# Output products of a recurrent attention kernel: accumulating by 128-column groups over all heads, without a sum over head groups

## The chip, the cores and the metric

The kernel runs on one core of a Trainium2 chip. The metric is the device time of one execution in microseconds (us); lower is better. Executions of one kernel differ by up to about 1% here. Ratios are the mean time of one kernel's runs over the mean of the other's of the same rounds, so they are not quite the ratio of the medians that are quoted beside them.

PE is the matmul engine, PEld its weight loads, DVE and ACT the vector and scalar engines that move results out of PSUM (the memory that matmuls write), SP the engine that issues DMA transfers.

## The reference, cut to what matters

It is a forward pass and its gradients. The part that matters is attention over segments of 32 rows with 8 memory rows, where each segment's memory comes out of the segment before it:

```python
mem = mem0                                           # 8 rows of 512
for s in range(n_seg):                               # 64 segments of 32 rows
    h = jnp.concatenate([mem, xs], axis=1)
    q, k, v = (jnp.einsum('btd,dhe->bhte', h, W) for W in (Wq, Wk, Wv))    # 32 heads of 128
    ...                                              # masked softmax of q k^T, times v
    o = jnp.einsum('bhte,hed->btd', o, Wo)           # the output product
    mem = o[:, :M, :].copy()                         # the next segment waits for this
```

So the forward pass is a chain of 64 steps, and the gradients go through a second chain of 64, from the last segment to the first. In a forward step the output product contracts 32 heads; in a backward step the corresponding product contracts 96 (q, k and v of 32 heads each).

## The kernel before

A step handles 32 rows. A matmul takes a stationary operand (here 128 x 32: one head's rows, transposed) and streams a moving one (a head's weights, here 128 x 512). The kernel runs four such matmuls side by side, each with its 32 columns in a column group of its own (in the trace before, four start within some 10 ns, and the next four 216 ns after the first). Before, the four groups hold four different heads, each streaming 512 columns:

```python
    def gather(R, XT, W, h, first, last):            # R: PSUM, 128 x 512 = (4 head groups x 32 rows) x 512
        for k in range(4 * h, 4 * h + 4):
            for g in range(HG):                      # HG = 4 head groups, KH = 8 heads in each
                nc.tensor.matmul(R[32 * g:32 * g + 32, :], lhsT=XT(k, g), rhs=W[:, g * KH + k, :],
                                 start=(first and k == 4 * h), stop=(last and k == 4 * h + 3),
                                 tile_position=(0, 32 * g))
```

The four groups then hold four partial sums, over eight heads each. A step ends with: `ra`, the copy of R (128 x 512) out of PSUM; `sm`, four fp32 matmuls with a 0/1 selection matrix, which add the four groups and leave the four 128-column pieces in four column groups; `sF`, a copy of the 128 x 128 result; `sT`, its transpose; `HT`, the copy of the memory rows into the next step's input.

```python
        def sm():
            ps["n"] = alloc("ps_sum")
            for c in range(DC):                      # DC = 4
                nc.tensor.matmul(ps["n"][SEG * c:SEG * c + SEG, 0:P], lhsT=sel[:], rhs=R4()[:, c * P:(c + 1) * P],
                                 start=True, stop=True, tile_position=(0, SEG * c), skip_group_check=True)
        def sF(): ...                                # PSUM -> SBUF, 128 x 128
        def sT(): ...                                # transpose on PE
```

The same form serves the "left-over rows" (the memory rows of four steps, handled once per block of four steps). Five stages follow each other: a dense part, the forward chain, a pass over the left-over rows ("lback"), the backward chain, and the weight gradients.

Of the kernel before, what the change touches and what calls it, by code (L numbers as in the profile page):

```python
# [8 lines left out]
ALU = mybir.AluOpType  # L9
AX = mybir.AxisListType  # L10
BF16 = mybir.dt.bfloat16
F32 = mybir.dt.float32
P = 128
# [13 lines left out]
def kernel(  # L27
# [27 lines left out]
    nc = tc.nc  # L55

    _, S, D = A_x.shape
    M = A_mem0.shape[1]
    H, Dh = A_Wq.shape[1], A_Wq.shape[2]
    F = B_w1.shape[1]  # L60
    SEG = int(A_seg_len)
    assert Dh == P and D % P == 0 and F % P == 0 and S % P == 0 and D <= 512
    L = M + SEG
    assert L <= 64 and P % SEG == 0
    NSEG = S // SEG
    DC = D // P
    TC = S // P
    HD = H * Dh
    SPB = P // SEG
# [28 lines left out]
    const = ctx.enter_context(tc.tile_pool(name="const", bufs=1))  # L98
# [3 lines left out]
    HG = 4  # L102
    KH = H // HG
# [48 lines left out]
    identF = const.tile([P, P], F32, name="identF")  # L152
    nc.vector.tensor_copy(identF[:], ident[:])

    sel = const.tile([P, SEG], F32, name="sel")
    nc.vector.tensor_reduce(sel[:], identF[:].rearrange("p (g r) -> p r g", g=HG), axis=AX.X, op=ALU.add)
# [15 lines left out]
    HT = htp.tile([P, DC, S], BF16, name="HT")  # L172
# [8 lines left out]
    jobs, lag = [], []  # L181
    with sb("p1", 1) as p1, sb("p1b", 2) as p1b:
# [81 lines left out]
        for rb in range(NRB):  # L264
# [4 lines left out]
            for fc in range(FC):  # L269
                ps = pst([P, RB], F32, name="ps_h1")  # L270
                for dc in range(DC):
                    nc.tensor.matmul(ps[:], lhsT=W1[:, dc, fc * P:(fc + 1) * P], rhs=HT[:, dc, r0:r0 + RB],
                                     start=(dc == 0), stop=(dc == DC - 1))
                nc.scalar.activation(rT[:, fc, :], ps[:], ACT.Relu, bias=b1T[:, fc:fc + 1], scale=1.0)
                nc.vector.tensor_tensor(out=aT[:, fc, :], in0=rT[:, fc, :], in1=rT[:, fc, :], op=ALU.mult)
            for fc in range(FC):
                ps2 = pst([P, RB], F32, name="ps_ga")
                for dc in range(DC):
                    nc.tensor.matmul(ps2[:], lhsT=W2T[:, dc, fc * P:(fc + 1) * P], rhs=gT[:, dc, r0:r0 + RB],
                                     start=(dc == 0), stop=(dc == DC - 1))  # L280
# [23 lines left out]
            for rc in range(RCB):  # L304
# [4 lines left out]
                for fc in range(FC):  # L309
                    nc.tensor.matmul(psB[:], lhsT=aT[:, fc, rc * P:(rc + 1) * P], rhs=W2[:, fc, :],  # L310
                                     start=(fc == 0), stop=(fc == FC - 1))
# [162 lines left out]
    def gather(R, XT, W, h, first, last):  # L474

        for k in range(4 * h, 4 * h + 4):
            for g in range(HG):
                nc.tensor.matmul(R[32 * g:32 * g + 32, :], lhsT=XT(k, g), rhs=W[:, g * KH + k, :],  # L478
                                 start=(first and k == 4 * h), stop=(last and k == 4 * h + 3),
                                 tile_position=(0, 32 * g))  # L480

    def sum_ops(o, alloc, R4, F, st, pre=""):

        ps = {}

        def sm():
            ps["n"] = alloc("ps_sum")
            for c in range(DC):
                nc.tensor.matmul(ps["n"][SEG * c:SEG * c + SEG, 0:P], lhsT=sel[:], rhs=R4()[:, c * P:(c + 1) * P],  # L489
                                 start=True, stop=True, tile_position=(0, SEG * c), skip_group_check=True)  # L490

        def sF():
            ps["F"] = F()
            ENGS[pre + "sF"](ps["F"][:], ps["n"][:, 0:P])

        def sT():
            nc.tensor.transpose(ps["n"][:, P:2 * P], ps["F"][:], identF[:])
            st["sum"] = ps["n"][:, P:2 * P].rearrange("p (c r) -> p c r", c=DC)
        o["sm"], o["sF"], o["sT"] = sm, sF, sT
# [92 lines left out]
    def play(order, n, steps, lefts, step, blk, last={}):  # L592
# [21 lines left out]
        "q1ev L.rc0 k1fl q0Te L.lq+ q1fl k0Te soP- k1Te s0 q1Te mx0 L.pm0 s1 km sb0 mx1 ex0 L.sm- soV- sb1 "  # L614
        "L.sF- soN ex1 v1mm ld- v0mm su0 rc0 su1 rc1 pm0 L.sT- ld tu0 pm1 tu1 kl+ v1ev L.lm v0ev L.ldL+ w0 "
        "L.xt- ob0 L.BT- oa0 L.rc1 soP L.tu0 w1 ob1 g0 oa1 g1 ra L.W0 sm L.out- L.oa0 sF L.ob0 sT HT",
        "k0mm L.hl++ L.pm1 q1mm q0mm ld k0ev xt- q1ev q0ev k1mm soV- k0fl q0fl L.tu1 k1ev k0Te q1fl q0Te k1fl k1Te s0 "
        "q1Te mx0 sb0 km s1 mx1 L.W1 ex0 sb1 su0 rc0 L.ob1 kl+ soN ex1 v0mm v0ev su1 L.oa1 v1mm pm0 rc1 tu0 w0 "
        "v1ev pm1 tu1 ob0 oa0 soV w1 ob1 g0 oa1 L.t3 g1 ra sm sF sT HT",
        "q0mm k0mm xt- q1mm k1mm q0ev q0fl q1ev k0ev soP- q0Te k0fl q1fl k1ev k1fl k0Te s0 q1Te k1Te mx0 L.u0- "  # L620
        "sb0 s1 v0mm mx1 sb1 ex0 ex1 su0 v0ev rc0 v1mm L.u3 su1 L.G0 rc1 pm0 pm1 L.t2 tu0 v1ev tu1 w0 ob0 L.t1 "
        "oa0 w1 g0 oa1 ob1 L.sx- L.ra0 L.u2 soP ld km g1 ra sm soN sF sT HT",
        "q0mm k0mm L.hs+ q0ev k1mm xt- q1mm q0fl k0ev kl q0Te k0fl k1ev k1fl L.u1 L.otr L.lo q1ev q1fl k0Te s0 k1Te "
        "q1Te mx0 s1 sb0 soV- ex0 L.t0 mx1 km sb1 su0 ex1 v1mm kl+ v0mm rc0 su1 rc1 pm0 tu0 L.mtr L.G1 v1ev "
        "v0ev pm1 tu1 L.lb w0 ob0 soN oa0 L.S0+ L.mx0+ w1 g0 oa1 ob1 g1 L.sb0+ ra L.ra1 sm sF L.S1+ sT HT")
    ENGS = on_engines(
        "L.oa0 L.oa1 L.ob0 L.ob1 L.sF L.xt k1Te k1ev oa1 ob0 q0ev q1ev ra v0ev v1ev",
        "HT L.pm0 L.pm1 L.ra0 k0Te k0ev oa0 ob1 pm0 pm1 q0Te q1Te sF xt")
    with sb("fw", 1) as fw, psum("fr", 4) as fr, psum("fpp", 1) as fpp, \
# [47 lines left out]
        def block(b):  # L677

            if b not in blk:
                shapes = {"kL": (fs, [P, KH, HG, NL], BF16), "OT": (fs, [P, HG, KH, SPB, SEG], BF16),  # L680
                          "X": (fs, [P, DC, P], BF16),
                          "kM": (fo, [P, KH, HG, NL], BF16), "vTM": (fo, [P, KH, HG, NL], BF16),
                          "XT": (fs, [P, DC, SPB, SEG], F32), "qL": (fo, [P, KH, HG, NL], BF16),
                          "VL": (fo, [P, GW], BF16), "vM": (fo, [P, GW], BF16), "EL": (fo, [P, KH, KW], BF16),
                          "OTL": (fo, [P, KH, HG, NL], BF16),
                          "bb": (fo, [P, D], BF16), "R4": (fo, [P, D], F32), "F": (fo, [P, P], F32)}

                def make(n):
                    pool, shape, dt = shapes[n]
                    return pool.tile(shape, dt, name=n, tag=n)  # L690
                blk[b] = Tiles(make)
            return blk[b]

        def left(b):

            B_ = block(b)
# [46 lines left out]
            o["ra0"] = lambda: ENGS["L.ra0"](B_["R4"][:], ps["R", 0][:])  # L743
            o["ra1"] = lambda: nc.vector.tensor_tensor(out=B_["R4"][:], in0=ps["R", 1][:], in1=B_["R4"][:], op=ALU.add)
            sum_ops(o, big, lambda: B_["R4"], lambda: B_["F"], st, "L.")
# [34 lines left out]
        def fwd(s):  # L780
# [80 lines left out]
            def ra():  # L861
                st["R4"] = fo.tile([P, D], F32, name="R4", tag="R4s")
                ENGS["ra"](st["R4"][:], ps["R"][:])
            o["ra"] = ra
            sum_ops(o, big, lambda: st["R4"], lambda: fo.tile([P, P], F32, name="F", tag="Fs"), st)
# [47 lines left out]
    with sb("ls", 3) as ls, sb("lo", 1) as lo_, psum("lpp", 1) as lpp, psum("lr", 4) as lr:  # L913
# [90 lines left out]
        "ra L.G1 sm vc sF L.H1 sT HT",  # L1004
        "L.ra1 o0mm ldk- o1mm o0ev vtr o0fl o0te vp0 veb0 xt- o1ev vlb0 vla0 L.ktr vea0 s0 o1fl vp1 o1te L.G2 "
        "d10 d20 veb1 s1 vlb1 d30 vg0 d40 vea1 tu0 ldq- vla1 kp0 vg1 d11 kea0 kla0 d21 klb0 keb0 d31 d41 L.vtr "
        "qp0 qeb0 ldp qea0 tu1 vc kg0 kp1 kea1 qg0 keb1 kla1 klb1 qp1 kg1 qeb1 qea1 qg1 L.H2 ra sm sF sT L.ra2 "
# [3 lines left out]
        "qp0 qeb0 qea0 tu1 kg0 kp1 kea1 keb1 qg0 kla1 klb1 qp1 L.qtr kg1 qeb1 qea1 qg1 ra L.H3 sm sF sT ldp ldn "  # L1011
        "HT",
        "L.ra3 o0mm L.qst o0ev L.ldt+ o1mm xt- o0fl L.gl+ o1ev vp0 o1fl o0te vlb0 vea0 vla0 s0 veb0 o1te vp1 "
        "d10 d20 d30 veb1 s1 d11 vg0 ldk- vlb1 d40 tu0 vea1 vtr L.gs+ vla1 ldq- d21 L.sm kp0 klb0 vc vg1 keb0 "
        "d31 L.sF kea0 kla0 d41 qp0 L.vo+ qeb0 tu1 kg0 qea0 L.ldv+ kp1 qg0 keb1 kla1 klb1 kea1 qp1 L.ldk+ qeb1 "
        "qea1 ldp kg1 L.ko+ qg1 ra sm sF L.sT sT HT")
    ENGS = on_engines(
        "L.ra0 L.sF kea0 kea1 kla0 kla1 o0ev o1ev o1te qea0 qeb1 ra sF vea0 vea1 veb1 vla0 vla1 vlb1 "
        "xt",
        "HT L.xt keb0 keb1 klb0 klb1 o0te qea1 qeb0 veb0 vlb0")  # L1020
    with sb("bq", 1) as bq, sb("bs", 2) as bs, sb("bt", 1) as bt, psum("bpp", 1) as bpp, psum("br", 4) as br:
# [11 lines left out]
        def block(b):  # L1033
            if b not in blk:
                shapes = {"gkL": (bs, [P, KH, HG, NL], BF16), "gvL": (bs, [P, KH, HG, NL], BF16),
                          "gqL": (bt, [P, KH, HG, NL], BF16), "PG": (bt, [P, 1, KH, KW], BF16), "GL": (bt, [P, 1, KH, KW], BF16),
                          "gOL": (bt, [P, GW], BF16), "qNL": (bt, [P, GW], BF16), "vTL": (bt, [P, KH, HG, NL], BF16),
                          "XT": (bs, [P, DC, SPB, SEG], F32), "R4": (bt, [P, D], F32), "F": (bt, [P, P], F32),
                          "gv": (bt, [P, HG, KH, SPB, SEG], BF16), "gk": (bt, [P, HG, KH, SPB, SEG], BF16),
                          "gq": (bt, [P, HG, KH, SPB, SEG], BF16)}  # L1040

                def make(n):
                    pool, shape, dt = shapes[n]
                    return pool.tile(shape, dt, name="b_" + n, tag=n)
                blk[b] = Tiles(make)
            return blk[b]

        def left(b):
# [15 lines left out]
            for i in range(4):  # L1064
                for x, nm in enumerate("GH"):
                    def G_(i=i, x=x):
                        if x == 0:
                            ps["R", i] = big("ps_RL")
                        for m, (W, n, k) in enumerate(jobs[6 * i + 3 * x:6 * i + 3 * x + 3]):
                            for g in range(HG):  # L1070
                                nc.tensor.matmul(ps["R", i][32 * g:32 * g + 32, :], lhsT=B_[n][:, k, g, :],  # L1071
                                                 rhs=W[:, g * KH + k, :], start=(x == 0 and m == 0),
                                                 stop=(x == 1 and m == 2), tile_position=(0, 32 * g))
                    o["%s%d" % (nm, i)] = G_
                if i == 0:
                    o["ra0"] = lambda: ENGS["L.ra0"](B_["R4"][:], ps["R", 0][:])
                else:
                    o["ra%d" % i] = lambda i=i: nc.vector.tensor_tensor(out=B_["R4"][:], in0=ps["R", i][:],
                                                                        in1=B_["R4"][:], op=ALU.add)
            sum_ops(o, big, lambda: B_["R4"], lambda: B_["F"], st, "L.")  # L1080
# [35 lines left out]
        def bwd(s):  # L1116
# [96 lines left out]
            def ra():  # L1213
                st["R4"] = bt.tile([P, D], F32, name="R4", tag="R4s")
                ENGS["ra"](st["R4"][:], ps["R"][:])
            o["ra"] = ra
            sum_ops(o, big, lambda: st["R4"], lambda: bt.tile([P, P], F32, name="F", tag="Fs"), st)
# [185 lines left out]
```

## Time and profile before

| what | value | from |
|---|---|---|
| median of the runs | 3284.57 us | 4 runs |
| forward chain | 937 us, granted clock 0.97 | windows |
| backward chain | 1047 us, granted clock 0.95 | windows |
| other three stages | 489, 177 and 618 us | first instructions of the stages |
| instruction packets, whole kernel | 406 | DMA queues |
| ... in the forward / backward chain | 147 / 199 | packet records of the trace |

PE and PEld together are 103,441 instructions (103,820 with the semaphore ones), and 103,820 / 406 = 256. So there is one packet of 16,384 bytes for every 256 PE instructions.

The windows view of the two chains of the kernel before (start and end in us, length, busy time with instruction counts of PE, PEld, DVE, ACT, POOL, granted clock, DMA share, GB/s):

```profile
488.80:1425.60 936.80, 769.93 (x18868) 406.36 (x18872) 509.71 (x1587) 381.72 (x833) 51.54 (x128) 0.97 0.67 169
1602.30:2649.20 1046.90, 867.16 (x25301) 417.15 (x25301) 435.90 (x1345) 384.21 (x1184) 89.66 (x128) 0.95 0.69 178
```

The timeline of PE at the end of one forward step of the kernel before (start, length, what, count, and in brackets the idle time before it with what ended it):

```profile
905.11 1.91 PE L478 MATMUL ps_R<-Wo,OT 128*32 128x512 bf16 x32
907.76 0.43 PE L489 MATMUL ps_sum<-R,sel 128*32 128x128 f32 x8 [0.74 <-ACT R L421]
908.61 0.33 PE L497 MATMUL ps_sum<-identF,F 128*128 128x128 f32 x1 [0.41 <-DVE F L424]
909.22 3.64 PE L437 MATMUL ps_proj<-Wqkv,X 128*32 128x512 bf16 x64 [0.28 <-DVE X L424]
```

PE stands idle for 0.74 us while ACT copies R. The waits of PE in the whole kernel before (what waited, for what, total us, times, longest):

```profile
PE l_pp L563 <- ACT l_gq L421: 71.1, 13, 15.1
PE ps_sum L489 <- ACT R L421: 53.0, 74, 0.8
PE b_pp L563 <- issue: 45.8, 34, 4.7
...
PE ps_gR L478 <- issue: 20.8, 16, 2.8
```

The second line is the wait that the change removes. The two lines "<- issue" are idle time that no semaphore explains; nearly all of it is in the backward chain (1.2 us in the forward one).

### The profile page before, as it was taken

To read this page: it belongs to the slowest core of one execution; us is meant where nothing else is said; L and a number is where in the kernel's file an instruction comes from. 1 tells how busy PE (TensorE), PEld (TensorE's weight loads), DVE (VectorE), ACT (ScalarE), POOL (GpSimd) and SP (SyncE) were. 2 spreads that over 40 slices of the span, in tenths; PEclk is the share of its full clock that TensorE was granted. 3 is DMA by queue.
4 is the path that set the end of the run, shared out by engine and by line. 5 is a ranking of instruction groups with operands and counts; after the bars stand their busy time and mean duration, and the time that the engine had idled before them with its cause. 6 is when DMAs were issued, how large, how long until landed. Compare 5 with 4: busy or idle time off the path is not lost.

```text
span 3266.8 us, 115469 instructions
## 1 busy us (share of the span) xinstructions
PE 2704.2 (83%) x51673; PEld 1338.9 (41%) x51768; DVE 1220.4 (37%) x3526; ACT 1017.1 (31%) x2492; POOL 193.7 (6%) x345
## 2 busy tenths in 40 slices
PE   8898778888888888834688888888888866999998
PEld 4453334444444444412344344344344423444444
DVE  4440035555655555523344344444444400010001
ACT  3331124444444444412333333333333401111111
POOL 0000000000000000000000010010000000000000
PEclk9999899999999999966799999999999988999999
DMA  9958894676667676689668666666776699999993
GB/s 254 283 145 312 293 291 114 165 179 162 185 164 184 161 184 161 171 235 256 185 164 210 166 164 181 189 164 172 190 183 172 173 260 199 205 186 224 187 187 91
DMA packets 890915, 633.20 MB, mean 194 GB/s; under 512 B 659745, under 2 KB 748466, under 8 KB 881074
## 3 DMA queue, kind: packets, MB, share of 16 engines
q1 hardware_dynamic: 890418, 625.81, 77.0%
q8 instruction: 406, 6.65, 0.8%
q14 instruction: 91, 0.75, 0.1%
HBM read 227.16 MB, written 250.10 MB: 146 GB/s over the span
## 4 chain that ended last, share of the span: by engine, by line
PE 57%; DMA 13%; SPq 13%; DVE 7%; issue 5%; ACT 5%; ACTq 0%; POOLq 0%; POOL 0%; DVEq 0%
PE ps_gR L478 11%; PE ps_proj L437 11%; PE ps_gw L1364 8%; SPq L1289 6%; PE b_pp L563 3%; PE ps_R L478 3%; DMA S_GOL<-l_gON 3%; PE ps_tr L167 2%; ACT R L421 2%; PE ps_sum L489 2%; PE ps_L L406 2%; DMA out_dram<-wt 2%; PE ps_w L366 2%; PE ps_w L386 1%; PE ps_RL L1071 1%
## 5 line engine op out<-in xcount | busy, mean ns | idle before, releaser
L1364 PE MATMUL ps_gw<-gn,HNc 128*128 128x512 bf16 x1881 | 416.5, 380 | 8.3 <-ACT wt L1339 6.3
L437 PE MATMUL ps_proj<-Wqkv,X 128*32 128x512 bf16 x6144 | 361.9, 385 | 18.2 <-DVE X L424 17.9
L1364 PEld LDWEIGHTS <-HNc 128*128 128x128 bf16 x1920 | 188.2, 98 | 231.9 <-issue 9.5
L421 ACT CAST f_N<-ps_proj 128x512 bf16<-128x512 f32 x320 | 185.4, 583 | 258.0 <-PE ps_proj L437 243.7
L1339 ACT CAST wt<-ps_gw 128x512 bf16<-128x512 f32 x126 | 69.5, 591 | 541.8 <-DMA out_dram<-wt 353.1
L437 PEld LDWEIGHTS <-X 128*32 128x32 bf16 x6144 | 156.9, 98 | 174.7 <-DVE X L424 29.9
L1322 DVE TENSOR_TENSOR gx<-ps_rows,gb 128x512 f32<-128x512 f32 x16 | 11.1, 692 | 427.5 <-PE ps_rows L1320 396.8
L1364 PE MATMUL ps_gw<-GOc,gn 128*128 128x512 bf16 x627 | 142.2, 387 | 19.2 <-DMA gn<-S_ON 18.3
L478 PE MATMUL ps_gR<-WT,b_gq 128*32 128x512 bf16 x2048 | 145.2, 401 | 7.8 <-issue 7.5
L478 PE MATMUL ps_gR<-WT,b_gk 128*32 128x512 bf16 x2048 | 145.8, 404 | 5.8 <-issue 5.7
L478 PE MATMUL ps_gR<-WT,b_gv 128*32 128x512 bf16 x2048 | 142.5, 393 | 7.6 <-issue 7.5
L437 PE MATMUL ps_proj<-WoT,GT 128*32 128x512 bf16 x2048 | 125.6, 388 | 22.5 <-DVE GT L424 17.9
L478 PE MATMUL ps_R<-Wo,OT 128*32 128x512 bf16 x2048 | 127.1, 390 | 0.0
L1145 POOL COPY b_vT<-b_vl 128x1024 bf16<-128x1024 bf16 x64 | 66.7, 1042 | 905.9 <-PE ps_sc L458 521.4
L421 ACT CAST gON<-ps_proj 128x512 bf16<-128x512 f32 x128 | 75.0, 586 | 118.9 <-PE ps_proj L437 115.2
L489 PE MATMUL ps_sum<-R,sel 128*32 128x128 f32 x1152 | 61.2, 285 | 58.4 <-ACT R L421 53.0
L1364 PEld LDWEIGHTS <-gn 128*128 128x128 bf16 x640 | 63.6, 100 | 96.4 <-DMA gn<-S_ON 18.6
L406 PE MATMUL ps_L<-Wqkv,XL 128*128 128x512 bf16 x376 | 84.8, 385 | 18.2 <-DMA XL<-S_XL 16.8
L421 ACT CAST b_gq<-b_pp 128x256 bf16<-128x256 f32 x128 | 47.7, 373 | 161.4 <-PE b_pp L563 153.3
L421 ACT CAST b_gk<-b_pp 128x256 bf16<-128x256 f32 x128 | 47.8, 373 | 150.7 <-PE b_pp L563 115.5
L424 DVE CAST b_gq<-b_pp 128x256 bf16<-128x256 f32 x128 | 54.4, 425 | 107.0 <-PE b_pp L563 102.8
L437 PEld LDWEIGHTS <-GT 128*32 128x32 bf16 x2048 | 49.5, 98 | 78.4 <-DVE GT L424 30.0
(214 smaller groups left out, 4427.9 us busy)
## 6 DMA issues: line engine op xcount, KB each, us to landing
S_A<-f_N SPq DMA_DIRECT2D x64, 512.0 KB
out_dram<-wt SPq DMA_DIRECT2D x154, 128.0 KB
S_A<-f_N SPq DMA_DIRECT2D x64, 256.0 KB
S_ON<-OC SPq DMA_DIRECT2D x64, 256.0 KB
b_qN<-S_A SPq DMA_DIRECT2D x64, 256.0 KB
b_kN<-S_A SPq DMA_DIRECT2D x64, 256.0 KB
S_GB<-b_gv SPq DMA_DIRECT2D x16, 1024.0 KB
S_GB<-b_gk SPq DMA_DIRECT2D x16, 1024.0 KB
```

The source lines that it names most:

```text
L167: nc.tensor.transpose(ps_ap, in_ap, ident[base:base + k, base:base + k])
L366: nc.tensor.matmul(ps[:], lhsT=aN[:, rc, fc * P:(fc + 1) * P], rhs=gN[:, rc, :], start=(rc == 0), stop=(rc == TC - 1))
L406: nc.tensor.matmul(ps[:], lhsT=XL[:, dc, q * P:(q + 1) * P], rhs=Wqkv[:, dc, c0:c0 + 512], start=(dc == 0), stop=(dc == DC - 1))
L421: nc.scalar.copy(out, in_)
L437: nc.tensor.matmul(ps[32 * g:32 * g + 32, :], lhsT=hT[:, dc, :], rhs=W[:, dc, c:c + 4 * P], start=(dc == 0), stop=(dc == DC - 1), tile_pos ...
L478: nc.tensor.matmul(R[32 * g:32 * g + 32, :], lhsT=XT(k, g), rhs=W[:, g * KH + k, :], start=(first and k == 4 * h), stop=(last and k == 4 * ...
L489: nc.tensor.matmul(ps["n"][SEG * c:SEG * c + SEG, 0:P], lhsT=sel[:], rhs=R4()[:, c * P:(c + 1) * P], start=True, stop=True, tile_position= ...
L563: nc.tensor.matmul(o, lhsT=N_[32 * g:32 * g + m, kk * P:(kk + 1) * P], rhs=X(kk)[32 * g:32 * g + m], start=(i == 0), stop=(i == len(jobs) ...
L1145: nc.gpsimd.tensor_copy(vT[:, :, :, 0:SEG], C["vl"][:])
L1289: nc.sync.dma_start_transpose(t_[:, b, :].rearrange("p (k e) -> p k e", k=KH), blocks(b)[:, g].rearrange("p k r -> p (k r)"))
L1339: nc.any.tensor_copy(wt[:], ps[:])
L1364: nc.tensor.matmul(ps[:], lhsT=l(rc), rhs=r(rc), start=(n == 0), stop=(n == RC_ALL - 1))
```

## The change

Its intent is to drop `ra` and `sm` from the end of every step. One head's rows go into all four column groups, and each group streams another 128 of that head's 512 columns. All 32 (or 96) heads then accumulate in one 128 x 128 area, already summed, and already in the layout that `sm` produced. The sum needs no matmul and the copy of R disappears. The core of the diff (the order lists lose `ra` and `sm`; the left-over rows get the same form; cuts marked):

```diff
     def gather(R, XT, W, h, first, last):
-        for k in range(4 * h, 4 * h + 4):
-            for g in range(HG):
-                nc.tensor.matmul(R[32 * g:32 * g + 32, :], lhsT=XT(k, g), rhs=W[:, g * KH + k, :],
-                                 start=(first and k == 4 * h), stop=(last and k == 4 * h + 3),
-                                 tile_position=(0, 32 * g))
-
-    def sum_ops(o, alloc, R4, F, st, pre=""):
...
-        def sm():
-            ps["n"] = alloc("ps_sum")
+        heads(R, [(W, XT(k, g), g * KH + k) for k in range(4 * h, 4 * h + 4) for g in range(HG)], first, last)
+
+    def heads(R, jobs, first, last):
+        for n, (W, x, h) in enumerate(jobs):
             for c in range(DC):
-                nc.tensor.matmul(ps["n"][SEG * c:SEG * c + SEG, 0:P], lhsT=sel[:], rhs=R4()[:, c * P:(c + 1) * P],
-                                 start=True, stop=True, tile_position=(0, SEG * c), skip_group_check=True)
+                nc.tensor.matmul(R[32 * c:32 * c + 32, 0:P], lhsT=x, rhs=W[:, h, c * P:(c + 1) * P],
+                                 start=(first and n == 0), stop=(last and n == len(jobs) - 1),
+                                 tile_position=(0, 32 * c))
...
-            def ra():
-                st["R4"] = fo.tile([P, D], F32, name="R4", tag="R4s")
-                ENGS["ra"](st["R4"][:], ps["R"][:])
+            def sF():
+                st["F"] = fo.tile([P, P], F32, name="F", tag="Fs")
+                ENGS["sF"](st["F"][:], ps["R"][:, 0:P])
...
```

The number of columns that the array streams stays the same. The number of matmuls, each with its own weight load, goes from one a head to four.

## The prediction

> **What bounds the kernel now.** The windows view puts the forward chain at about 500-1400 us and the backward chain at about 1600-2640 us, 64 steps each (about 13.8 and 16.2 us a step), with PE busy about 85% in both. In the chain of waits a forward step is projections, scores, softmax, products, then the tail: output product (32 matmuls of 128x512, 1.9 us), R eviction on ACT 0.59, head-group sum 0.47, F eviction 0.30, transpose 0.34, HT copy 0.20.
>
> **Removed.** The 512-column eviction and the sum: 0.59 + 0.47 us and three hand-overs, about 1.2 us of every one of 128 steps. The timeline shows PE idle 0.74 us before the sum, so it is on the path: about 150 us gross.
>
> **Moved.** Each head's product is 4 matmuls of 128 columns in place of one of 512, in the same four column groups. Today four 128x512 matmuls with different column groups start 3.3 ns apart, one such round each 215.8 ns. The 128-column transposes start 55.8 ns apart at best, and scores (40 columns, column groups) show rounds of 26 ns including their weight loads, so I expect rounds of about 56 ns: 32 heads 1.79 us instead of 1.73. Over 10,240 heads that is about 20 us lost. By PE streaming alone the change would win about 100-130 us.
>
> **Added: instructions.** 10,240 heads x 3 more pairs of weight load and matmul, less 1,280 pairs of the sum: +58,900 PE instructions on 103,800. The instruction queue's 406 packets of 16,384 B are one per 256 PE instructions. In this trace successive fetches are never under 3.29 us apart, with a crowd at 3.3-3.6, though one takes only 1.0 us of DMA. [...] in the backward chain PE stops some twenty times for 1.5-4.8 us without a semaphore wait, each time ended by one instruction packet landing about 1.3 us earlier; together about 55 us. [...] From the moment a block is entered to the next being usable I read about 3.5 us typically, over 5.5 us one time in six, 3.6-4.0 us on average.
>
> Backward, a step goes from about 790 to 1,490 PE instructions: 5.8 blocks, so at least 20-22 us where it is 16.2 now. Forward: about 3.2 blocks, 11.5-12.5 us, against a chain that would take 12.7: its gain is about consumed by stalls where small matmuls crowd. Replaying the recorded spacing of PE instructions with these edits and a serial fetch of 3.3-4.0 us per block gives (estimates): forward +15 to +75 us, backward +290 to +480 us. The gain in the chain is thus more than lost: instruction fetch becomes the bound of the backward chain.
>
> **Predicted: 3730 us, range 3540 to 3890. Faster by over 2%: 0.08; within 2%: 0.05; slower by over 2%: 0.87.**
>
> **What would show each step.** About 635 instruction packets. In the backward chain, fetches 3.3-4 us apart nearly all the time; PE idle by "issue" (no releaser) of several hundred us, in mid-gather; backward windows with lower PE busy. The gather's rounds at about 56 ns between stalls. From gather's end to the transpose about 0.8 us instead of 1.9. First, second (lback) and last stages unchanged.
>
> **What would make it wrong.** If fetches can overlap when demanded faster, the stalls shrink and the kernel lands at 3150-3250 us. If the weight loads of four column groups are not hidden behind 128-column matmuls, [...] that, not fetch, sets the time. Fewer delayed fetches, as DMA load per us falls, would put it at 3600.

3730 us is the kernel before with a forward chain longer by 15 to 75 us and a backward chain longer by 290 to 480, together 305 to 555 (about 3590 to 3840 us in all). The "serial fetch" of the replay is my assumption, and its 3.3 to 4.0 us an estimate from the intervals between packets: in the trace before, no packet starts before the one ahead of it has ended (none of 405), and the shortest interval between two starts is 3.29 us.

## More of the kernel before

The profile page of the kernel before starts so: busy time of PE, then slices of the span (each digit is tenths busy), then the granted clock of PE in tenths, and the queue that brings instructions.

```profile
PE 2704.2 (83%) x51673; PEld 1338.9 (41%) x51768; DVE 1220.4 (37%) x3526; ACT 1017.1 (31%) x2492; POOL 193.7 (6%) x345
...
PE   8898778888888888834688888888888866999998
...
PEclk9999899999999999966799999999999988999999
...
q8 instruction: 406, 6.65, 0.8%
```

Most of the two chains (slices 7 to 17 and 21 to 32) show PE busy in eight tenths.

The profiled execution of the kernel before took 3268.5 us, some 16 us below its median time; stage times come from it, so their differences below add up to about 20 us more than the difference of the medians.

## The result, and the profile after

The changed kernel takes 3965.68 us (median of 4 runs, 3961.65 to 3971.2) against 3284.57: ratio 1.2071, 95% interval 1.2048 to 1.2094. It is slower, as forecast, but by 681 us where 445 were forecast, and outside the forecast range. All outputs are right.

| stage | before us | after us | difference | packets before | packets after |
|---|---|---|---|---|---|
| dense part | 489 | 491 | +2 | 18 | 18 |
| forward chain | 937 | 1061 | +124 | 147 | 202 |
| lback | 177 | 180 | +3 | 21 | 21 |
| backward chain | 1047 | 1610 | +563 | 199 | 374 |
| weight gradients | 618 | 628 | +10 | 21 | 21 |

The same parts of the page of the changed kernel:

```profile
PE 2964.5 (75%) x81113; PEld 1842.7 (46%) x81208; DVE 1199.8 (30%) x3525; ACT 930.1 (23%) x2332; POOL 195.1 (5%) x345
...
PE   8988877787878784556666666666666766599998
...
PEclk9999989898999896678877778778877788799999
...
q8 instruction: 636, 10.42, 1.1%
```

PE is busy longer in total but for a smaller share of the span, and its granted clock is lower. The windows view of its two chains:

```profile
490.60:1551.80 1061.20, 820.63 (x25908) 505.01 (x25912) 496.59 (x1587) 342.54 (x753) 51.22 (x128) 0.89 0.60 150
1731.60:3341.20 1609.60, 1071.72 (x47700) 820.04 (x47700) 428.74 (x1345) 336.52 (x1104) 91.27 (x128) 0.79 0.48 117
```

PE's idle time in the backward chain is 1609.6 - 1071.7 = 538 us, where it was 180. The clock falls to 0.79, and the DMA share falls too, so neither PE's own work nor the transfers of data seem to set the pace. The end of a forward step does what the change intended. The timeline of PE there, in the changed kernel (the window cuts off the first products of the call):

```profile
902.76 1.27 PE L479 MATMUL ps_R<-Wo,OT 128*32 128x128 bf16 x37
904.42 0.47 PE L487 MATMUL ps_sum<-identF,F 128*128 128x128 f32 x1 [0.39 <-DVE F L421]
905.18 5.21 PE L434 MATMUL ps_proj<-Wqkv,X 128*32 128x512 bf16 x64 [0.28 <-DVE X L421]
```

From the end of the products to the transpose it is 0.39 us instead of 1.59. But the 64 projections after it take 5.21 us, not 3.64: the granted clock was at half until 908.4 us. Over the 64 forward steps the median of these projections is 4.60 us, against 3.64 before. The waits of PE in the whole changed kernel:

```profile
PE ps_gR L479 <- issue: 263.2, 178, 4.9
PE b_pp L553 <- issue: 113.3, 75, 4.2
PE ps_R L479 <- issue: 96.7, 53, 3.4
PE l_pp L553 <- ACT l_gq L418: 73.3, 15, 13.0
PE ps_RL L479 <- issue: 67.9, 44, 3.1
```

The wait for R is gone. In its place, lines "<- issue", which were 67 us in the largest two, are 541 us in these four. A stretch of the backward chain shows what they are: 58 of 64 products of one call run, then PE stops for 3.61 us, and the last six of the same call follow.

```profile
2024.64 1.01 PE L479 MATMUL ps_gR<-WT,b_gv 128*32 128x128 bf16 x58
2029.26 0.40 PE L479 MATMUL ps_gR<-WT,b_gv 128*32 128x128 bf16 x6 [3.61 <-issue]
```

Nothing that these six read is missing: the 58 before them read the same tiles. What comes just before PE goes on is an instruction packet. I counted PE instructions against the packets of the instruction queue in the trace. In the backward chain of the changed kernel 335 of 374 blocks of 256 instructions end with PE stopped, for 1.68 us on average, at the same place in the count each time. (Such counts depend on the shortest pause that counts as a stop: 327 to 338 here for 0.3 to 0.1 us.) In these, PE goes on 1.24 to 1.57 us (5th to 95th percentile) after the end of one packet. The packet itself starts 1.2 us (median) after PE has entered the block before, and takes 1.1 us. No packet of this trace starts before the one ahead of it has ended (none of 635; the shortest interval between two starts is 3.24 us), so I take the packet to be what PE waits for in these stops.

### The profile page after: what moved, and what is told of

It is laid out like the page before. It is cut to its first block, busy times and chain, and to the rows that moved or that the text cites. A ratio compares the mean times of both kernels' runs of the same rounds, so it can differ in the third digit from the quotient of the medians. Undisturbed runs are those within 1.5% of the kernel's fastest.

```text
span 3969.4 us, 174201 instructions
## 1 busy us (share of the span) xinstructions
PE 2964.5 (75%) x81113; PEld 1842.7 (46%) x81208; DVE 1199.8 (30%) x3525; ACT 930.1 (23%) x2332; POOL 195.1 (5%) x345
## 4 chain that ended last, share of the span: by engine, by line
PE 57%; issue 17%; SPq 9%; DMA 8%; DVE 6%; ACT 2%; ACTq 0%; POOLq 0%; POOL 0%; DVEq 0%
PE ps_gR L479 14%; PE ps_proj L434 12%; PE ps_gw L1352 8%; SPq L1277 4%; PE ps_R L479 4%; PE b_pp L553 3%; PE ps_RL L479 3%; PE ps_tr L164 2%; DMA S_GOL<-l_gON 2%; DMA out_dram<-wt 1%; PE ps_w L363 1%; PE ps_w L383 1%; PE f_pp L553 1%; PE ps_sum L487 1%; PE ps_L L403 1%
## 5 line engine op out<-in xcount | busy, mean ns | idle before, releaser
L434 PE MATMUL ps_proj<-Wqkv,X 128*32 128x512 bf16 x6144 | 412.3, 422 | 23.0 <-DVE X L421 17.9
L479 PE MATMUL ps_gR<-WT,b_gk 128*32 128x128 bf16 x8192 | 217.0, 275 | 88.1 <-issue 87.8
L479 PE MATMUL ps_gR<-WT,b_gq 128*32 128x128 bf16 x8192 | 218.1, 275 | 75.2 <-issue 74.9
L479 PE MATMUL ps_gR<-WT,b_gv 128*32 128x128 bf16 x8192 | 164.0, 231 | 100.5 <-issue 100.4
L479 PE MATMUL ps_R<-Wo,OT 128*32 128x128 bf16 x8192 | 153.8, 234 | 96.7 <-issue 96.7
L479 PEld LDWEIGHTS <-b_gk 128*32 128x32 bf16 x8192 | 174.0, 124 | 109.1 <-issue 104.6
L479 PEld LDWEIGHTS <-b_gq 128*32 128x32 bf16 x8192 | 182.0, 126 | 89.2 <-issue 87.3
L434 PE MATMUL ps_proj<-WoT,GT 128*32 128x512 bf16 x2048 | 159.1, 456 | 43.0 <-issue 20.7
L479 PEld LDWEIGHTS <-b_gv 128*32 128x32 bf16 x8192 | 129.8, 102 | 110.3 <-issue 107.7
L479 PEld LDWEIGHTS <-OT 128*32 128x32 bf16 x8192 | 131.9, 104 | 105.2 <-issue 103.2
```

What stands on the lines that cost most here:

```text
L434: nc.tensor.matmul(ps[32 * g:32 * g + 32, :], lhsT=hT[:, dc, :], rhs=W[:, dc, c:c + 4 * P], start=(dc == 0), stop=(dc == DC - 1), tile_pos ...
L479: nc.tensor.matmul(R[32 * c:32 * c + 32, 0:P], lhsT=x, rhs=W[:, h, c * P:(c + 1) * P], start=(first and n == 0), stop=(last and n == len(j ...
```

## The experiments

Theory F, read from these counts: PE's instruction stream is fetched one block of 256 at a time, about 3.3 us at the shortest (3.29 us between packets in the trace before, 3.24 in the one after); wherever PE uses up 256 instructions faster, it waits, and the change quadruples the instructions of the products. Rival W: the new arrangement or the narrow matmul itself is what costs (one head in all four column groups, 128 columns at a time, four times the weight loads).

### split4: the additional instructions without the new arrangement

The kernel before, with each product cut into four of 128 columns in the same column group. `ra`, `sm` and all of the data flow stay.

```diff
+        w = 128
         for k in range(4 * h, 4 * h + 4):
-            for g in range(HG):
-                nc.tensor.matmul(R[32 * g:32 * g + 32, :], lhsT=XT(k, g), rhs=W[:, g * KH + k, :],
+            for q in range(0, D, w):
+                for g in range(HG):
+                    nc.tensor.matmul(R[32 * g:32 * g + 32, q:q + w], lhsT=XT(k, g), rhs=W[:, g * KH + k, q:q + w],
...
```

> The kernel before, with each 128x512 output product cut into four of 128 columns in the same column group; data flow, eviction and sum of head groups as before. Theory F (the PE instruction stream is fetched one 256-instruction block at a time, about 4.2 us a block when it is behind): about 646 instruction packets, forward 1080-1150 us, backward 1600-1700, total 3980-4120 us, granted clock about 0.86. Rival W (the loss comes from the new arrangement: one head's rows in all four column groups, accumulating in 128 columns of PSUM): under 3350 us, since that arrangement is absent here.

Measured: 4130.09 us (2 runs), ratio 1.2577 (1.2509 to 1.2645); forward 1178 us, backward 1654, 646 packets. That is 10 us above F's range in total and 28 above in the forward chain, and far from W's. The arrangement of the change is not needed for the loss. The waits of PE in split4:

```profile
PE ps_gR L480 <- issue: 249.2, 176, 4.6
PE b_pp L565 <- issue: 107.9, 69, 3.9
PE ps_R L480 <- issue: 98.6, 52, 4.0
...
PE ps_sum L491 <- ACT R L421: 52.3, 74, 0.7
```

The same "<- issue" lines as in the changed kernel stand beside the wait for R of the kernel before. The difference between split4 and the changed kernel also gives an upper bound for what the change wins: 4130 - 3966 = 164 us, in the traces 117 forward and 44 backward. Up to 43 us of this are the 1,280 more pairs of the sum (10 packets of about 4.3 us), and 20 us are projections that took longer at a lower granted clock (431.8 us busy in split4, 412.3 in the changed kernel). So the shorter chain is worth some 100 to 160 us where the fetch is the bound (an estimate, and not measured apart), and the additional instructions cost about 850.

### loads7: additional instructions without narrow matmuls (a test that does not decide)

Six more weight loads of the same rows before each 512-column product.

```diff
+                for _ in range(6):
+                    nc.tensor.ldweights(XT(k, g), tile_position=(0, 32 * g))
                 nc.tensor.matmul(R[32 * g:32 * g + 32, :], lhsT=XT(k, g), rhs=W[:, g * KH + k, :],
...
```

> The kernel before, with six more weight loads of the same 32 columns ahead of each 128x512 output product, so that the number of PE instructions grows by 61,440 (the change: 58,880) while no matmul becomes narrow and nothing is rearranged. F: about 646 instruction packets and 3950-4150 us, most blocks 3.3-4.5 us apart. Rival W, or a rival by which narrow matmuls cost the array or PSUM more: 3280-3400 us. A rival by which the weight loads themselves are what costs would also give a long time, but with gather rounds longer than 216 ns between stalls and no idle time that a fetch ends.

Measured: 4840.3 us (2 runs), ratio 1.474 (1.4654 to 1.4826), 646 packets, clock 0.937. The forecasts of F and W missed; what came is the last rival of the expectation, that the weight loads themselves cost. Seven weight loads in a row are not hidden behind one matmul: a call of 16 products in the backward chain takes 2.32 us where it took about 1.09, and PE became the bound, so that the fetch had 5.6 us a block and hardly mattered (PE pauses for over 0.15 us at the end of 44 of the 379 backward blocks). This kernel says nothing for or against F. It does say that weight loads cost when they are stacked, which made the next test necessary: is one load hidden for each 128-column matmul?

### narrow_grads: the same cut where the fetch has room

In the last stage the kernel before runs 2,560 matmuls of 128 x 512, with few instructions per us (21 packets in 618 us). They are cut into four of 128 columns, each with its own weight load of 128 columns.

```diff
-                        nc.tensor.matmul(ps[:], lhsT=l(rc), rhs=r(rc), start=(n == 0), stop=(n == RC_ALL - 1))
+                        for q in range(0, 512, P):
+                            nc.tensor.matmul(ps[:, q:q + P], lhsT=l(rc), rhs=r(rc)[:, q:q + P],
+                                             start=(n == 0 and q == 0), stop=(n == RC_ALL - 1), skip_group_check=True)
```

> The kernel before, with the 2,560 matmuls of 128x512 of the last stage (weight gradients) cut into four of 128 columns each: the same cut as in the change, where the instruction stream has room. +15,360 PE instructions, 60 blocks, so about 80 packets in 620 us, 7.8 us a block. F: nothing stalls; matmuls start about 56 ns apart, the stage grows by 3 to 6%, 15-40 us, total 3295-3330 us. Rival W (128-column matmuls or their additional weight loads cost the array by themselves): [...] the stage grows by 250-500 us.

Measured: 3302.58 us (2 runs), ratio 1.0071 (1.0028 to 1.0115); the stage grows from 618 to 657 us with 81 packets. Groups of PE instructions of the kernel before (total busy, mean ns of one, idle before), then of narrow_grads:

```profile
L1364 PE MATMUL ps_gw<-gn,HNc 128*128 128x512 bf16 x1881 | 416.5, 380 | 8.3 <-ACT wt L1339 6.3
```

```profile
L1365 PE MATMUL ps_gw<-gn,HNc 128*128 128x128 bf16 x7680 | 437.4, 220 | 15.0 <-ACT wt L1339 15.0
```

Four times the matmuls cost 3 to 5% more busy time (1,881 of the 1,920 wide ones are in the record) and no wait for issue in this group. In the trace's records the matmuls start 55.8 ns apart for hundreds at a time. So a 128-column matmul with its own load is not slow by itself, when its instructions are there. The 32-column form of the change agrees: where the changed kernel's products run without a stop, they start 14.0 ns apart on average, 56 ns for a round of four column groups. Together with split4 this removes W.

### fwd_only and bwd_only: the stages separately

The change in one chain, the kernel before in the other.

> The change in the forward stage alone (steps and left-over rows). F with the stage times of the two traces: forward about 1060 us as in the changed kernel, backward about 1047 as before, total 3390-3430 us. If the loss were one common cost that appears only with both stages changed: forward below 937 us and a faster kernel, about 3210.

Measured: 3388.88 us (4 runs), ratio 1.0333 (1.0284 to 1.0382), 1 us below the expected range; forward 1043, backward 1051.

> The change in the backward stage alone. F: forward 937, backward about 1610, total 3820-3880 us, about 580 instruction packets.

Measured: 3840.57 us (2 runs), ratio 1.1696 (1.1637 to 1.1754); forward 944, backward 1608, 581 packets.

The two losses over the kernel before of the same rounds, 108 and 560 us, add up to 668; the whole change loses 681. The stages are independent, and the change does not pay in either.

### split2: a smaller dose

As split4, with two pieces of 256 columns.

> The kernel before, with each output product cut into two of 256 columns in the same column group: half of the dose of split4 in additional instructions would be two thirds; this is one third (20,480). F: forward about 167 blocks, 945-1010 us; backward about 259 blocks of 4.2-4.6 us, 1110-1250 us; total 3370-3560 us, PE stalled at the end of more than half of the backward blocks. If the cost were in proportion to instructions, as a fixed cost of each: a third of split4's +849 us, 3560. If only 128-column matmuls are slow: under 3330.

Measured: 3457.3 us (2 runs), ratio 1.0543 (1.0499 to 1.0587); forward 967, backward 1195, 486 packets. It is inside F's ranges (4.61 us a block is at the edge of 4.2 to 4.6); a fixed cost of each instruction would have given 3560, and "only 128 columns are slow" under 3330. With late_both (below) this gives a series for the backward chain, from the packet records and my count of stops:

| kernel | packets in the backward chain | backward us | us per packet | blocks that end with PE stopped |
|---|---|---|---|---|
| before | 199 | 1047 | 5.26 | 46% |
| late_both | 223 | 1056 | 4.74 | 58% |
| split2 | 259 | 1195 | 4.61 | 67% |
| after | 374 | 1610 | 4.30 | 90% |
| split4 | 379 | 1654 | 4.36 | 85% |

The percentages of the last column shift with the shortest pause that counts as a stop, most for the kernel before (34 to 44% for pauses from 0.3 to 0.1 us that end just after a packet). The time per packet is not under 4.30 us in any of the five, and near that each additional packet costs nearly as much (from split2 to split4: 459 us for 120 packets, 3.8 us each; from split2 to after 3.6, with the shorter chain counted in). Where there is more time per packet, one costs less: the forward chain of split2 (967 us) has 20 more packets than the 147 before (6.4 us each), for 30 us. late_both has 24 more in its backward chain, for 9 us, but its chain no longer has the wait for R, which took 14.1 us there before.

### more_dma: what sets the time of a fetch

The changed kernel, with one additional copy of 1 MB in DRAM in each backward step. Nothing waits for it.

```diff
+    S_EXTRA = dram.tile([NSEG, P, HD], BF16, name="S_EXTRA")
...
                 def mm(p=p):
+                    if p == 0:
+                        dma(S_EXTRA[s], S_WOT[:, s % DC, :])
```

> The changed kernel with one additional copy of 1 MB from DRAM to DRAM in each backward step (64 MB more, nothing waits for it). It asks why a fetch takes 4.15-4.26 us a block there and not the 3.4-3.6 of the shortest. Theory Q (the tail of the fetch time, start of the packet 1.7-4 us after the block is entered instead of 1.1-1.2, is queueing behind other transfers): the mean backward interval of fetches rises from 4.26 to 4.5 us or more, backward 1700 us or more, total above 4050. Otherwise: mean interval within 0.1 us of 4.26 and total 3940-4000.

Measured: 4111.34 us (2 runs), ratio to the kernel before 1.2538 (1.2485 to 1.259); backward 1768 us with the same 374 packets, all as theory Q forecast. In the trace's packet records, the intervals between starts of instruction packets in the backward chain changed like this:

```
                 5%     25%    median   75%    95%    mean
after            3.41   3.59   3.91     4.51   6.57   4.25
more_dma         3.38   3.62   3.96     5.52   7.43   4.68
```

The short half of the intervals does not move; the long quarter does. The share of packets that start more than 3 us after PE entered the block before went from 10% to 23%. So the long intervals grew with 64 MB more of other transfers (95% point 6.57 to 7.43 us), and the short ones did not (5% point 3.41 and 3.38, 25% point 3.59 and 3.62). That it is queueing, as theory Q has it, was not shown: no run here shows a queue.

### late_fwd, late_both, ra_two, mix: attempts at a version that gains

If instructions are the price, pay it only where it shortens the chain. In late_fwd the second half of the forward heads is accumulated in the new form; the first half goes as before, `ra` runs beside the second half's products, and `sm` adds into the same bank.

```diff
+                    XT = lambda k, g: B_["OT"][:, g, k, j, :]
                     if "R" not in ps:
                         ps["R"] = big("ps_R")
-                        ps["n"] = 0
-                    ps["n"] += 1
-                    gather(ps["R"], lambda k, g: B_["OT"][:, g, k, j, :], Wo, p, ps["n"] == 1, ps["n"] == 2)
+                        gather(ps["R"], XT, Wo, p, True, True)
+                    else:
+                        ps["S"] = big("ps_sum")
+                        heads(ps["S"], XT, Wo, p)
...
-        "... w1 ob1 g0 oa1 g1 ra L.W0 sm L.out- L.oa0 sF L.ob0 sT HT",
+        "... w1 ob1 g0 oa1 ra g1 L.W0 sm L.out- L.oa0 sF L.ob0 sT HT",
```

> The kernel before with the column-group form for the second half of the forward step's heads alone (16 heads, 48 more pairs a step): the first half goes as before, is evicted while the second half runs, and its head-group sum accumulates into the second half's bank. F: about 171 forward blocks, few stalls; the 0.74 us of PE idle before the sum goes: forward 885-920 us, total 3225-3265. If any use of the column-group form slows the product (rival W): forward above 937.

Measured: 3285.77 us (6 runs), ratio 1.0027 (0.9998 to 1.0055): the same as before, and F's forecast of 3225 to 3265 missed. (Forward 943 us is in W's range, above 937, but the new form's products show no slowdown that would make it so: 64 of them take 1.07 us, 16 wide ones 1.05.) The timeline of PE shows that the step's end did become shorter; the sum follows without an idle gap:

```profile
907.89 1.05 PE L478 MATMUL ps_R<-Wo,OT 128*32 128x512 bf16 x16
908.76 1.07 PE L487 MATMUL ps_sum<-Wo,OT 128*32 128x128 bf16 x64
909.68 0.43 PE L498 MATMUL ps_sum<-R,sel 128*32 128x128 f32 x8
```

The forward steps come in blocks of four. Their medians went from 14.5, 13.5, 13.7 and 13.6 us (first to fourth step of a block) to 16.0, 13.0, 12.8 and 14.2: the second and third fell, the first and fourth rose. The forward stage took 943 us. PE's wait for R there is gone (38.9 us before), but its waits for issue rose from 1 us to 19 in the three largest lines, those for the value rows that are loaded for the next step from 6.7 to 15.6 us, and PE was busy 13 us longer (782.6 against 769.9, at a granted clock of 0.95 against 0.97). So the gain was given back to the fetch, to transfers and to longer busy time.

> As late_fwd, and in the backward step the last 16 of 96 products too. F: backward about 247 blocks in the stage, near the rate of the fetch, so what the chain gains (about 45 us) goes into stalls: backward 1030-1090 us, total 3220-3300, no better than late_fwd. Without a fetch limit: backward about 1000, total about 3190.

Measured: 3290.32 us (6 runs), ratio 1.0038 (1.0002 to 1.0075); backward 1056. As forecast, it is no better than late_fwd.

ra_two copies R in two halves on two engines, with no additional PE instruction (`acp(R4[:, 0:256], R[:, 0:256])` and `vcp` for the other half in place of one copy).

> The kernel before with the eviction of R cut in two halves, one on ACT and one on DVE: the chain is shortened by about 0.17 us a step with not one PE instruction more. If a shorter chain alone pays: 128 x 0.17 = 22 us, total 3255-3270. If gains of the chain are taken back by transfers and fetches at block boundaries, as late_fwd suggests: 3270-3285.

Measured: 3305.52 us (6 runs), ratio 1.0082 (1.0055 to 1.0108): slower than either forecast; forward 955 us, backward 1062. The trace shows why: the two halves ran one after the other. In the timeline of a forward step DVE starts when ACT has ended, and PE's eight matmuls of the sum wait for it midway:

```profile
918.73 0.37 ACT L421 COPY R<-ps_R 128x256 f32<-128x256 f32 x1 [1.49 <-PE ps_R L478]
919.14 0.42 DVE L424 COPY R<-ps_R 128x256 f32<-128x256 f32 x1 [1.79 <-ACT R L421]
919.15 0.87 PE L489 MATMUL ps_sum<-R,sel 128*32 128x128 f32 x8 [0.53 <-ACT R L421]
```

In the median of the 64 steps of each chain the sum ended 1.40 us after the products, where it was 1.17 before. The chain became longer by 0.23 us a step, 30 us in 128 steps, which is about what was lost. So this run did not shorten the chain and says nothing on what a shorter one is worth.

mix has late_fwd's forward stage with the value-row load of a block's first step moved to that step's start, and ra_two's copy in the backward stage.

> late_fwd's forward stage with the load of the value rows for the first step of a block issued at that step's start instead of its middle, and ra_two's eviction in the backward stage. If the forward gain of late_fwd (0.9 us in ordinary steps) was given back to that load (14.3 us of PE waiting against 5.7) and to fetch stalls (about 21 us): forward 925-938, total 3250-3275; if it was the fetch alone: 3270-3290.

Measured: 3288.08 us (6 runs), ratio 1.0027 (0.9994 to 1.006). Forward 934 us, inside the forecast and 9 less than late_fwd in single traces: the wait for the value rows is gone, but that for the memory's value rows (vM) went from 10.3 to 19.1 us. Backward took 1061, 14 more than before, as ra_two's longer copy lets expect; so the total missed the first forecast. No version here beats the kernel before.

## Why the prediction was right or wrong

**Right: the direction and the bound.** The forecast named the fetch of PE instructions as the new bound of the backward chain, from the intervals between packets and some twenty unexplained stops in the trace before. split4, narrow_grads and split2 show it. The counts were right: about 635 packets forecast, 636 measured; +58,900 PE instructions forecast, 58,894 measured. Rounds of about 56 ns were forecast and 56 measured, weight loads included. From the products' end to the transpose 1.1 us less were forecast (0.8 instead of 1.9) and 1.2 measured (0.39 instead of 1.59).

**Wrong: the size of one fetch.** The prediction says "about 3.5 us typically, over 5.5 us one time in six, 3.6-4.0 us on average" and replays the instruction spacing with "a serial fetch of 3.3-4.0 us per block". This is the step that failed. In the changed kernel a block that ends with a stop takes 4.15 us on average, and the backward chain 4.30 us per packet (1609.6 us over 374). With 3.8 us a packet the chain would take 1421 us, so this term alone is about 190 of the missing 236 us. The size was misread in two ways:

- The fetch did not become slower than it was in the trace before. There, over the 199 backward blocks, the time from entering a block to the next being usable (an estimate: the end of its packet and the 1.4 us until PE goes on) has a median of 3.8 us, is over 5.5 us in 15% and has a mean of 4.4 us; in the changed kernel the mean is 4.2. The prediction's own words, 3.5 us and over 5.5 us one time in six, already give at least 3.8, and its replay used fixed values about the typical one. A fixed value leaves out, as I see it, that a late packet costs its whole delay while an early one saves nothing (my estimate; no run shows it apart).
- Fewer delayed fetches were expected, since the DMA load per us would fall. It did fall (share 0.69 to 0.48), but delayed packets (more than 3 us after the block was entered) only went from about 15% to 10%. In more_dma, where the share was 0.54 to 0.59 (three windows from 1800 to 3000 us, 0.47 in the changed kernel), it is 23%: there more load went with more delayed packets.

**Missing: the clock.** The prediction contains no change of the granted clock. It fell from 0.943 to 0.857, in the forward chain from 0.97 to 0.89. The trace's clock records hold two values only, full and half, 46 stretches at half before and 155 after. The half clock begins 89 times in the backward chain of the changed kernel. In its records 309 of 310 stretches last a multiple of 3.41 us. Of the 819 steps of 3.41 us at full clock in the whole changed kernel 154 are followed by half clock: none in which PE was idle for less than 1.17 us in total, and every one with more than 2.01 us. So in this trace the fall of the clock goes with the stops; no run changes the clock alone.

In the backward chain slower matmuls probably fill, for the most part, time that the fetch takes anyway (my estimate, not shown). In the forward chain they lie in the recurrence: the projections' busy time rose from 361.9 to 412.3 us. There the measured terms nearly close: idle time for issue about +123 us (the waits of that stage), projections +50, output products 127.1 to 153.8 us, +27; less the wait for R (39), the sum's matmuls (34) and a shorter wait for F (7), which gives +120 where the chain lost 124. Without the longer projections and products the loss would have been about 47 us, inside the 15 to 75 that were forecast; so the missing clock term is most of the forward miss.

**Half right: the gain.** "About 1.2 us of every one of 128 steps ... about 150 us gross" is within the 100 to 160 us that split4 bounds, but not in the way it was argued. The wait for R occurs in 74 steps, 55 of them forward and 19 backward (in the others PE has left-over rows to work on meanwhile), and the gain is mostly forward (at most 117 us against 44). That 150 us comes so near is in part luck. In late_fwd a gain of 0.5 to 0.9 us in half of the forward steps moved the total by nothing.

**Unchanged stages.** Forecast as unchanged, measured +2, +3 and +10 us.

## What to carry to other kernels

Count instructions, not only columns and bytes: before cutting one matmul into four, divide PE's instructions of each stage by those of one packet (here 256) and compare the time per block with the shortest interval between instruction packets in the trace (here 3.29 us before the change; in the backward chain after it 4.30 us a packet on average). Here 64 narrow products with their loads, half a block, took 1.07 us in late_fwd, so a block of them would take about 2.1 us (an estimate from that figure). A stage that already shows idle time without a releaser, in the middle of one call, was near that limit (the backward chain before, 5.26 us a packet), and a shorter chain there bought nothing (late_both: 9 us lost in the backward chain). And when replaying a trace with a limit whose delays vary, use the recorded spread of delays, not its typical value.
